# Attention scores over all 128 rows of the array, with high parts of the keys over low parts, and all stages of two tiles

## The chip, the cores and the metric

The kernel runs on one core of one Trainium2 chip. The metric is the device time of one execution in microseconds (us), lower being better. The core's engines, by the short names of the profile, are PE (TensorE; its weight loads are listed apart as PEld), DVE (VectorE), ACT (ScalarE), POOL (GpSimd) and SP (which issues most of the transfers here). A change of about 2% is what a measurement of this kernel can tell from no change.

## The reference

Three layers follow one another on 1536 tokens of width 512 (2 batches of 768 positions, 8 heads of 64).

```python
# 1. attention: local window (n_local = 96) plus the first n_global = 8 keys, with a slope per head
scores = q @ k.T / 8 - slope[h] * dist          # slope[h] = 2 ** -(h + 1); others masked
a = softmax(scores);  attn = a @ v
# 2. gated layer
xn = x / rms(x) * rms_g
x = (silu(xn @ w_gate) * (xn @ w_val)) @ w_out  # float64 weights, 512 x 1536
# 3. one expert of 8 per token
e = argmax(x @ gate);  p = softmax(x @ gate)[e]
out = p * (relu(x @ w1[e]) @ w2[e])             # 512 x 1024, 1024 x 512
```

## The kernel before

**Split numbers.** Products run on PE in a rounded float format. To keep float32 precision an operand is stored as a high part (the rounded value, written by ACT or DVE) and a low part (the value less its high part, written by DVE or POOL). A product is then the sum of three: high by high, high by low, low by high. This holds for the scores (`qt`, `kt`), for the gated layer (`gv`, `ow` are weights, `xn` is the input, `hid` the hidden layer) and for the experts (`ew`, `eh`, `xs`).

**Tiles and stages.** A tile is 128 tokens. `SPLIT` cuts the 12 tiles into stages: three of 2 tiles for the first batch, two of 3 tiles for the second. Attention goes stage by stage, and in a stage by pair of heads (`order`): a group is one stage of one pair, so there are 20 groups. A unit is one tile of a group: 48 units. When the four groups of a stage are done, `tail` normalizes and transposes its tiles (`trx`), and `moe_block(0, ...)` of that stage (its first 3 of 12 slices of the gated layer) may be put between later attention units. After attention the loops `moe_block(1, ...)` (slices 3 to 6) and `moe_block(2, ...)` (slices 7 to 11) run over all stages; the products of a slice (`pg`) take the whole stage as their moving operand, 256 columns wide for 2 tiles and 384 for 3. The last loop ends each stage with `route`, which picks the expert. For the first `NDL` = 4 stages `route` computes its logits on DVE, 16 operations `jk` a tile; for later ones on PE, by transposes `trr` and products `lg`. Then come the experts.

**A group's preparation** (`prep`) is put into the program one group ahead. The natural keys `kn` and queries `qn` lie with the first head of the pair on partitions 0 to 63 and the second on 64 to 127. ACT writes the high keys (line 423), POOL the low keys (line 426; DVE in the first two groups), ACT or DVE the scaled high queries (433 or 429), DVE the low queries (434). POOL then builds with small copies (line 394) the windows with the global keys in front. `kt` and `qt` have two buffers each.

**A unit's scores** (`scores`, line 482) are three products a head, each over the 64 partitions of that head:

```python
seq = list(enumerate(((0, 0), (0, 1), (1, 0))))
r = slice(D * j, D * (j + 1))
lhsT=qt[r, a, t * P:(t + 1) * P], rhs=kt[r, c, ...]
```

DVE adds the distance table to each head's scores and takes the maximum (line 489), ACT takes the exponential (493), PE transposes the result (`pp`, line 504), ACT copies it out of PSUM (512), and PE multiplies it with the values (`xp`, line 533). Meanwhile DVE, ACT and POOL also convert the float64 weights of the gated layer (`cv`, lines 302 to 322).

**Order.** The engines run their queues in program order. A scheduler sets that order when the program is built, from the order of the source and what depends on what; the order below is the built one. `warm` products do no work for the result and are put where PE would idle at the start.

Of the kernel before, what the change touches and what calls it, by code (L numbers as in the profile page):

```python
# [8 lines left out]
F32 = mybir.dt.float32  # L9
F32R = mybir.dt.float32r  # L10
# [3 lines left out]
ACTF = mybir.ActivationFunctionType  # L14
ALU = mybir.AluOpType
# [4 lines left out]
P = 128  # L20
B, H, S, D = 2, 8, 768, 64
NT, DM, DFF = B * S, H * D, 1536
# [23 lines left out]
def kernel(  # L46
# [22 lines left out]
    M0 = [3, 3, 3, 3, 3]  # L69
    M1 = 7  # L70
    PM = [[0, 1, 2], [3, 4, 5, 6], [], [7, 8], [9], [10, 11]]
    NHID = 6
# [59 lines left out]

    gB = const.tile([P, DM], F32, name="gB")
    rg = const.tile([P, KD, NE], F32, name="rg")
    qsc = const.tile([P, NP], F32, name="qsc")
    for hp in range(NP):
        for j in range(2):
            h = 2 * hp + j
            nc.gpsimd.memset(qsc[64 * j:64 * j + 64, hp:hp + 1], 0.125 / slope[h])

    tri_f = const.tile([P, P], F32, name="tri_f")
    nc.gpsimd.memset(tri_f, 1.0)
    nc.gpsimd.affine_select(
# [55 lines left out]
    def load_pair(st, hp, kn, qn, vn):  # L199
        b, t0, nt = STARTS[st] // TB, STARTS[st] % TB, SIZES[st]  # L200
        i0 = 0 if t0 else 1
        nk = nt + 1 - i0
        k0 = (t0 - 1 + i0) * P
        hd = slice(P * hp, P * (hp + 1))
        nc.sync.dma_start(out=kn[:, i0 * P:(nt + 1) * P], in_=kT[b][hd, k0:k0 + nk * P])
        nc.sync.dma_start(out=qn[:, 0:nt * P], in_=qT[b][hd, t0 * P:(t0 + nt) * P])
        nc.sync.dma_start(
            out=rows_of(vn)[:, i0:i0 + nk, 1:P + 1],
            in_=v[b, k0:k0 + nk * P, hd].rearrange("(t p) c -> p t c", p=P),
        )  # L210
        return kn, qn, vn
# [39 lines left out]
    nc.vector.tensor_copy(tab0, tabL[:, P:])  # L251
    nc.vector.tensor_tensor(out=tab0[:, :GW], in0=tab0[:, :GW], in1=gcol, op=ALU.max)
    nc.vector.tensor_tensor(out=tabL[:, :GW], in0=tabL[:, :GW], in1=gcol, op=ALU.max)

    warm(WARM0)
    fast = nc.values_load(flag, min_val=0, max_val=1)

    def body(is_fast):
# [127 lines left out]
        def fast_attention(pool):  # L386
# [9 lines left out]
            def prep(gi):  # L396
                st, hp = order[gi]
                t0, nt = STARTS[st] % TB, SIZES[st]
                i0 = 0 if t0 else 1
                n = nt * P  # L400
                kn, qn, vn = loaded.pop(0)
                vn = rows_of(vn)
                nc.gpsimd.memset(vn[:, i0:nt + 1, 0:VW:VW - 1], 1.0)
                nxt = range(NFP, NFP + 2) if gi == 0 else range(gi + 2, gi + 3) if gi >= NFP else ()
                for gn in nxt:
                    if gn >= len(order):
                        break
                    nat = [
                        pool.tile([P, STAGE if x == "q" else DM if x == "k" else (ST_MAX + 1) * VW], F32, tag=f"{x}n", bufs=2, name=f"{x}n") for x in "kqv"
                    ]  # L410
                    loaded.append(load_pair(*order[gn], *nat))
                qt = pool.tile([P, 2, STAGE], F32R, tag="qt", bufs=2, name="qt")
# [3 lines left out]
                src = kn[:, i0 * P:(nt + 1) * P]  # L416
                khi = kt[:, 0, OW + i0:OW + nt + 1, :].rearrange("p t n -> p (t n)")
                klo = kt[:, 1, OW + i0:OW + nt + 1, :].rearrange("p t n -> p (t n)")
                hi_dve = HI[gi >= HIN]
                if hi_dve[0]:  # L420
                    nc.vector.tensor_copy(khi, src)
                else:
                    nc.scalar.activation(out=khi, in_=src, func=ACTF.Copy)  # L423
# [3 lines left out]
                srq = qn[:, 0:n]  # L427
                if hi_dve[1]:
                    nc.vector.tensor_scalar(
                        out=qt[:, 0, 0:n], in0=srq, scalar1=qsc[:, hp:hp + 1], scalar2=None, op0=ALU.mult  # L430
                    )
                else:
                    nc.scalar.activation(out=qt[:, 0, 0:n], in_=srq, func=ACTF.Copy, scale=qsc[:, hp:hp + 1])
                lo_eng[kq[1]].scalar_tensor_tensor(
                    out=qt[:, 1, 0:n], in0=srq, scalar=qsc[:, hp:hp + 1], in1=qt[:, 0, 0:n].bitcast(F32),
                    op0=ALU.mult, op1=ALU.subtract,
                )
# [12 lines left out]
                mx = pool.tile([P, ST, 2], F32, tag="mx", bufs=3, name="mx")  # L450
                groups.append((st, t0, hp, qt, kt, vn, vx, mx))
# [3 lines left out]
            def scores(g, t):  # L455
                st, t0, hp, qt, kt, vn, vx, mx = groups[g]
                if SB:
                    sb = ps("s", NS, "sp")
                    sp = [sb[:, 0:256], sb[:, 256:512]]
                else:  # L460
                    sp = [ps("s", NS, "sp") for _ in range(2)]
                first = t0 + t == 0
                plain = t0 + t == 1
                n = P if first else 256
                tab = tab0 if first else tabL if plain else tabG
                pr = pool.tile([P, 2, 256], F32, tag="pr", bufs=NPR, name="pr")
                OW = ST_MAX
                seq = list(enumerate(((0, 0), (0, 1), (1, 0))))
                for i, a, c, j in (
                    [(i, a, c, j) for j in range(2) for i, (a, c) in seq] if SB else  # L470
                    [(i, a, c, j) for i, (a, c) in seq for j in range(2)]
                ):
                    r = slice(D * j, D * (j + 1))
                    o = sp[j][:, 0:n]
                    if first:
                        rhs = kt[r, c, OW + 1, :]
                    elif plain:
                        rhs = kt[r, c, OW + t:OW + t + 2, :].rearrange("p t n -> p (t n)")
                    else:
                        rhs = kt[r, c, t:t + OW + 2:OW + 1, :]  # L480
                        o = o.rearrange("p (a n) -> p a n", a=2)
                    mm = nc.tensor.matmul(  # L482
                        out=o, lhsT=qt[r, a, t * P:(t + 1) * P], rhs=rhs, start=(i == 0), stop=(i == 2)
                    )
                un = units.index((g, t))
                if un < WARMU:
                    warm(WARM2[un % len(WARM2)], mm)
                for j in range(2):
                    nc.vector.tensor_tensor_reduce(  # L489
                        out=pr[:, j, 0:n], in0=sp[j][:, 0:n], in1=tab[:, 0:n], scale=-slope[2 * hp + j],  # L490
                        scalar=3.0e38, op0=ALU.add, op1=ALU.min, accum_out=mx[:, t, j:j + 1],
                    )
# [803 lines left out]
```

## Time and profile before

| what | value |
|---|---|
| median of 3 runs | 718.35 us (706.99 to 719.83) |
| the profiled execution | 715.3 us |
| its span, first to last instruction | 713.5 us |
| mean granted clock of TensorE, share of full speed | 0.921 |
| busy: PE, DVE, ACT, POOL | 94%, 63%, 44%, 44% of the span |

The span leaves 1.8 us of the profiled execution outside. A busy share is a mean over stages that differ. A busy PE is not a PE at its peak, since the profile's matmuls overlap and a product waiting inside the array counts as busy.

### The profile page before, as it was taken

The numbers are of one execution on the slowest core, as the hardware profiler recorded it, in microseconds if no ns is written. First come the engines' busy times: TensorE is split into PE (matmuls) and PEld (weight loads), VectorE is DVE, ScalarE is ACT, GpSimd is POOL, SyncE is SP. The second block draws the span as 40 slices with busy tenths as digits, with TensorE's granted clock in tenths as the row PEclk, the third lists the DMA queues.
The fourth block names the chain that finished last, engine by engine and source line by source line (L and its number), as shares of the span: only waits on it lengthen the run. The fifth ranks groups of instructions, "written<-read, shape, count | busy, mean of one in ns | idle before, by whom it ended". The sixth has DMA issues, their size and how long they took to land. (4 is left out here: it accounts for less than half of the span.)

```text
span 713.5 us, 11325 instructions
## 1 busy us (share of the span) xinstructions
PE 669.8 (94%) x4008; PEld 589.9 (83%) x4009; DVE 452.1 (63%) x1249; ACT 312.5 (44%) x594; POOL 310.5 (44%) x343
## 2 busy tenths in 40 slices
PE   7999999999999799999889999988898999999992
PEld 3778988888898698899789999977687888998891
DVE  5667577675479999524447999796546455536410
ACT  2566467675554444222541212131445465555420
POOL 3445444452034555222331323452578586777400
PEclk7555599999999999999999999998999999999997
DMA  6334224140004443200421110233276666676201
GB/s 218 102 109 131 68 72 122 62 145 16 16 8 141 121 145 120 88 0 1 138 99 60 60 60 0 61 87 105 79 262 228 206 221 214 198 230 212 88 12 28
DMA packets 49079, 77.29 MB, mean 108 GB/s; under 512 B 6127, under 2 KB 30703, under 8 KB 49008
## 3 DMA queue, kind: packets, MB, share of 16 engines
q1 hardware_dynamic: 46064, 69.07, 31.1%
q0 software_dynamic: 2944, 7.35, 3.1%
q8 instruction: 35, 0.57, 0.4%
q14 instruction: 36, 0.29, 0.1%
HBM read 70.06 MB, written 7.40 MB: 109 GB/s over the span
## 5 line engine op out<-in xcount | busy, mean ns | idle before, releaser
L701 PE MATMUL pg<-xn,gv 128*128 128x256 f32 (+1 forms) x1440 | 225.1, 311 | 10.2 <-DVE part L747 6.1
L701 PEld LDWEIGHTS pg<-xn,gv 128*128 128x128 f32 x1440 | 213.7, 194 | 15.9 <-DVE part L747 6.7
L738 PE MATMUL po<-ow,hid 128*128 128x512 f32 x432 | 111.2, 406 | 8.1 <-DVE hf L714 3.5
L888 POOL TENSOR_TENSOR ew<-rawe,ew 128x512 fp32r<-128x512 f32 x64 | 99.5, 1568 | 43.0 <-ACT ew L882 42.5
L719 POOL TENSOR_TENSOR hid<-hf,hid 128x256 fp32r<-128x256 f32 (+1 forms) x60 | 57.2, 956 | 122.3 <-ACT hid L718 121.8
L885 DVE TENSOR_TENSOR ew<-rawe,ew 128x512 fp32r<-128x512 f32 x64 | 68.4, 1076 | 65.3 <-ACT ew L882 64.7
L738 PEld LDWEIGHTS po<-ow,hid 128*128 128x128 f32 x432 | 80.9, 193 | 26.2 <-issue 3.8
L942 PE MATMUL py<-ew,eh 128*128 128x512 f32 x384 | 92.7, 399 | 4.1 <-DVE eh L973 3.1
L882 ACT ACTIVATE ew<-rawe 128x1024 fp32r<-128x1024 f32 x64 | 66.7, 1061 | 65.1 <-DMA rawe<-in_moe_w_dram 55.0
L942 PEld LDWEIGHTS py<-ew,eh 128*128 128x128 f32 x384 | 72.4, 191 | 21.3 <-DVE eh L973 3.6
L964 PE MATMUL ph<-xs,ew 128*128 128x256 f32 x672 | 83.3, 282 | 0.8 <-DVE eh L973 0.6
L964 PEld LDWEIGHTS ph<-xs,ew 128*128 128x128 f32 x672 | 81.3, 190 | 1.9 <-DVE eh L973 1.2
L771 DVE CUSTOM_DVE_ANT_0 jk<-part,rgb 128x256 bf16<-128x256 f32 x144 | 71.0, 535 | 0.0
L718 ACT ACTIVATE hid<-hf 128x256 fp32r<-128x256 f32 (+1 forms) x60 | 27.4, 459 | 87.9 <-DVE hf L714 87.8
L493 ACT ACTIVATE pr<-pr,mx 128x256 f32<-128x256 f32 (+1 forms) x96 | 44.7, 484 | 28.5 <-DVE mx L489 26.3
L482 PE MATMUL sp<-kt,qt 64*128 64x256 f32 (+1 forms) x288 | 54.6, 372 | 1.5 <-ACT kt L423 0.8
L322 POOL TENSOR_TENSOR gv<-cv,gv 128x512 fp32r<-128x512 f32 x24 | 31.9, 1335 | 54.6 <-ACT gv L321 54.6
L482 PEld LDWEIGHTS sp<-kt,qt 64*128 64x128 f32 x288 | 38.2, 238 | 17.3 <-DVE mx L489 3.6
L709 ACT ACTIVATE th<-pg 128x256 f32<-128x256 f32 (+1 forms) x60 | 25.1, 420 | 50.7 <-PE pg L701 49.5
L710 DVE SCALAR_TENSOR_TENSOR th<-th,pg 128x256 f32<-128x256 f32 (+1 forms) x60 | 28.0, 468 | 28.4 <-ACT th L709 28.4
L489 DVE CUSTOM_DVE_ANT_0 pr<-sp,tabG 128x256 f32<-128x256 f32 x64 | 26.2, 421 | 27.5 <-PE sp L482 25.6
L504 PE MATMUL pp<-ident,pr 128*128 128x128 f32 x176 | 39.5, 335 | 0.0
(173 smaller groups left out, 867.0 us busy)
## 6 DMA issues: line engine op xcount, KB each, us to landing
rawe<-in_moe_w_dram SPq DMA_DIRECT2D x64, 512.0 KB, 4.0
raw<-in_moe_w_gate_dram SPq DMA_DIRECT2D x12, 512.0 KB, 3.7
raw<-in_moe_w_val_dram SPq DMA_DIRECT2D x12, 512.0 KB, 3.6
raw<-in_moe_w_out_dram SPq DMA_DIRECT2D x12, 512.0 KB, 3.5
x1d<-part SPq DMA_DIRECT2D x12, 256.0 KB, 2.1
kn<-in_k_dram SPq DMA_DIRECT2D x12, 192.0 KB, 2.6
vn<-in_v_dram SPq DMA_DIRECT2D x12, 192.0 KB, 2.6
rawg<-in_moe_w_gate_dram SPq DMA_DIRECT2D x4, 512.0 KB, 4.6
```

What stands on the lines that cost most here:

```text
L482: mm = nc.tensor.matmul(out=o, lhsT=qt[r, a, t * P:(t + 1) * P], rhs=rhs, start=(i == 0), stop=(i == 2))
L493: pin["act"] = nc.scalar.activation(out=pr[:, j, 0:n], in_=pr[:, j, 0:n], func=ACTF.Exp, bias=mx[:, t, j:j + 1], scale=-1.0,)
L504: nc.tensor.transpose(pp[:, (j * nb + a) * P:(j * nb + a + 1) * P], pr[:, j, a * P:(a + 1) * P], ident)
L701: nc.tensor.matmul(out=pg[:, 0:n_], lhsT=gv[:, i, a, kk, :], rhs=x[st][:, kk, :], start=(n == 0), stop=(n == 3 * KD - 1),)
L719: nc.gpsimd.tensor_tensor(out=hh[:, 1], in0=hf, in1=hh[:, 0].bitcast(F32), op=ALU.subtract)
L738: nc.tensor.matmul(out=po, lhsT=hid[mi][:, a, t * P:(t + 1) * P], rhs=ow[:, c, :], start=(mi == 0 and n == 0), stop=(mi == len(ms) - 1 and ...
L771: nc.vector.tensor_tensor_reduce(out=jk, in0=part[i0 + t][:, h * 256:(h + 1) * 256], in1=rgb[h][:, e, :], scale=1.0, scalar=0.0, op0=ALU.m ...
L882: cp = nc.scalar.activation(out=t[:, 0], in_=raw, func=ACTF.Copy)
L885: nc.vector.tensor_tensor(out=t[:, 1, 0:NDV], in0=raw[:, 0:NDV], in1=t[:, 0, 0:NDV].bitcast(F32), op=ALU.subtract)
L888: nc.gpsimd.tensor_tensor(out=t[:, 1, NDV:], in0=raw[:, NDV:], in1=t[:, 0, NDV:].bitcast(F32), op=ALU.subtract)
L942: last_mm["py"] = nc.tensor.matmul(out=py, lhsT=hid(m, a, j), rhs=w2t[m // 2][:, c, (m % 2) * DM:(m % 2 + 1) * DM], start=(n == 0), stop=( ...
L964: nc.tensor.matmul(out=ph[:, 0:CAP], lhsT=w1t[kk][:, a, m * P:(m + 1) * P], rhs=x[:, kk, :], start=(n == 0), stop=(n == 3 * KD - 1),)
```

## The change

The scores of a head use all 128 partitions. Both natural tiles are loaded twice, onto partitions 0 to 63 and again onto 64 to 127, and hold the two heads side by side along the free axis. High keys are written on all 128 partitions, and on the lower 64 of them (64 to 127) the low keys are then written over them. One product of a high query (which stands on both halves) with this column gives high by high plus high by low. The second product is the low query with the same column: it gives low by high, and also low by low, which was left out before. So a head takes two products in place of three, and the pieces are no longer tied to half of the array's rows. Since both heads now share one factor, the queries are scaled by a constant, and a halved copy of each distance table is made for the second head (three ACT operations at the start).

`SPLIT` becomes six stages of 2 tiles, so there are 24 groups and 48 units as before. All `pg` products are 256 wide: 864 of 256 and 576 of 384 columns become 1728 of 256. With `NDL` still 4, `route` works on DVE for 8 tiles (9 before) and on PE for 4 (3 before). Buffers follow: `XT`, `RING` and `FIRST` are rewritten, and the pool `eb` has two buffers in place of three, so that the ring of expert weights keeps twelve.

```diff
-SPLIT = [[2, 2, 2], [3, 3]]
+SPLIT = [[2, 2, 2], [2, 2, 2]]
...
-    XT = "cccss"
-    RING = "ccceewwee"
-    FIRST = [0,1,1,2]
+    XT = "ccccss"
+    RING = "ccceewweec"
+    FIRST = [0, 1, 1, 1, 1]
...
-        nc.sync.dma_start(out=kn[:, i0 * P:(nt + 1) * P], in_=kT[b][hd, k0:k0 + nk * P])
-        nc.sync.dma_start(out=qn[:, 0:nt * P], in_=qT[b][hd, t0 * P:(t0 + nt) * P])
+        for x, src in ((kn[:, 0:2 * nk * P], kT[b][hd, k0:k0 + nk * P]), (qn[:, 0:2 * nt * P], qT[b][hd, t0 * P:(t0 + nt) * P])):
+            for r in range(2):
+                nc.sync.dma_start(
+                    out=x[D * r:D * (r + 1), :].rearrange("d (j s) -> d j s", j=2),
+                    in_=src.rearrange("(j d) s -> d j s", j=2),
+                )
...
+    tabs = []
+    for x in (tab0, tabL, tabG):
+        half = const.tile([P, x.shape[1]], F32, name="half" + str(len(tabs)))
+        nc.scalar.activation(out=half, in_=x, func=ACTF.Copy, scale=0.5)
+        tabs.append((x, half))
...
-                lo_eng[kq[0]].tensor_tensor(out=klo, in0=src, in1=khi.bitcast(F32), op=ALU.subtract)
+                lo_eng[kq[0]].tensor_tensor(out=ks[D:P], in0=src[D:P], in1=ks[D:P].bitcast(F32), op=ALU.subtract)
...
-                seq = list(enumerate(((0, 0), (0, 1), (1, 0))))
-                for i, a, c, j in (
-                    [(i, a, c, j) for j in range(2) for i, (a, c) in seq] if SB else
-                    [(i, a, c, j) for i, (a, c) in seq for j in range(2)]
-                ):
-                    r = slice(D * j, D * (j + 1))
+                for j, a in ((0, 0), (0, 1), (1, 0), (1, 1)):
...
-                        out=o, lhsT=qt[r, a, t * P:(t + 1) * P], rhs=rhs, start=(i == 0), stop=(i == 2)
+                        out=o, lhsT=qt[:, j, a, t * P:(t + 1) * P], rhs=rhs, start=(a == 0), stop=(a == 1)
...
-        ring["pools"] += [(eb, "ew", 3, GV)] * 3
+        ring["pools"] += [(eb, "ew", 2, GV)] * 2
```

The built order shows where the pieces stand. On PE, in the part of attention that has no gated layer beside it yet, the program before has this (`sp` are scores, `pp` transposes):

```order
L504 MATMUL pp<-ident,pr 128x128 x2
L482 MATMUL sp<-kt,qt 128x256 x3
L504 MATMUL pp<-ident,pr 128x128 x4
L482 MATMUL sp<-kt,qt 128x256 x6
L504 MATMUL pp<-ident,pr 128x128 x2
```

And the changed program has this at the corresponding place on PE:

```order
L485 MATMUL sp<-kt,qt 128x256 x2
L507 MATMUL pp<-ident,pr 128x128 x6
L485 MATMUL sp<-kt,qt 128x256 x4
L536 MATMUL xp<-vx,ptS 128x65
L536 MATMUL xp<-vn,ptS 128x65
```

A unit's six score products stood as one piece of six or as two pieces of three (73 pieces for the 48 units); now its four stand as four, or two and two.

On POOL, in the second and third stage, one group's preparation before (the low keys, then windows of keys and values):

```order
L426 TENSOR_TENSOR kt<-kn,kt 128x384
L394 TENSOR_SCALAR kt<-kg 128x2x2x32
L394 TENSOR_SCALAR kt<-kt 128x2x2x96
L403 MEMSET vn 128x3x2
L394 TENSOR_SCALAR vx<-vn 128x260
```

And on POOL in the changed program:

```order
L399 TENSOR_SCALAR kt<-kg 128x2x2x32
L408 MEMSET vn 128x3x2
L399 TENSOR_SCALAR vx<-vn 128x260
L432 TENSOR_TENSOR kt<-kn,kt 64x2x384
L399 TENSOR_SCALAR vx<-vg 32x2x128
L399 TENSOR_SCALAR kt<-kt 128x2x2x96
```

The low keys now are 64 partitions of 768 elements in place of 128 of 384, and stand among the copies of values, with the copy of the windows behind them.

On PE, at the end of the last loop over stages, before: the fourth stage's products and, in the fifth stage's output products `po`, the ranks `rk` of the fourth.

```order
L701 MATMUL pg<-xn_220,gv_3928 128x384 x24
L738 MATMUL po<-ow_3020,hid 128x512 x3
L738 MATMUL po<-ow_3099,hid 128x512 x3
L738 MATMUL po<-ow_3885,hid 128x512 x3
L738 MATMUL po<-ow_3917,hid 128x512
L827 LDWEIGHTS tri
L827 MATMUL rk<-oh,tri 128x16
```

And on PE in the changed program, where the fifth of six stages is routed (`trr`, `lg`) among the sixth one's `pg`:

```order
L831 MATMUL rk<-oh,ones 128x16
L789 MATMUL trr<-ident,part_119 128x128 x4
L704 MATMUL pg<-xn_224,gv_3186 128x256 x12
L789 MATMUL trr<-ident,part_120 128x128 x4
L704 MATMUL pg<-xn_224,gv_4142 128x256 x10
L801 MATMUL lg<-rg,xt 128x8 x4
L704 MATMUL pg<-xn_224,gv_3107 128x256 x12
```

One more stage's logits moved to PE, and `pg` products of the last stage stand between their steps.

## Rows read from the trace of the kernel before

**Rows 1.** Windows: span, busy per engine, granted clock, DMA share, GB/s.

```profile
10.70:89.20 78.50, 77.88 (x336) 61.54 (x335) 51.70 (x169) 44.16 (x97) 33.02 (x56) 0.50 0.41 125
89.20:190.00 100.80, 100.80 (x743) 87.39 (x742) 68.36 (x254) 65.72 (x145) 38.18 (x72) 1.00 0.25 77
190.00:300.00 110.00, 101.44 (x627) 93.77 (x627) 90.67 (x151) 50.15 (x101) 48.12 (x41) 0.97 0.32 101
...
400.00:420.00 20.00, 20.00 (x145) 18.81 (x144) 19.93 (x84) 4.72 (x12) 7.41 (x8) 1.00 0.14 50
```

**Rows 2.** Windows of line 482 alone (scores): span, PE busy, PEld busy, clock, DMA.

```profile
10.70:89.20 78.50, 26.55 (x118) 19.24 (x118) 0.50 0.41 125
89.20:190.00 100.80, 27.72 (x168) 18.79 (x168) 1.00 0.25 77
```

**Rows 3.** Timeline of PE at the half clock: start us, length us, what, count.

```profile
58.44 1.01 PE L482 MATMUL sp<-kt,qt 64*128 64x256 f32 x3
...
62.70 0.63 PE L533 MATMUL xp<-vn,ptS 128*128 128x65 f32 x2
63.13 0.63 PE L504 MATMUL pp<-ident,pr 128*128 128x128 f32 x2
63.69 1.02 PE L482 MATMUL sp<-kt,qt 64*128 64x256 f32 x6
64.64 0.69 PE L504 MATMUL pp<-ident,pr 128*128 128x128 f32 x2
```

**Rows 4.** Timeline of the weight loads there, idle before them in brackets.

```profile
60.42 0.72 PEld L482 LDWEIGHTS sp<-kt,qt 64*128 64x128 f32 x6 [0.33 <-POOL kt L394]
```

**Rows 5.** Timeline of PE at the full clock.

```profile
110.86 0.39 PE L533 MATMUL xp<-vn,ptS 128*128 128x65 f32 x2
111.09 0.61 PE L376 MATMUL trx<-ident,part 128*128 128x128 f32 x4
111.62 0.62 PE L482 MATMUL sp<-kt,qt 64*128 64x256 f32 x6
112.17 0.44 PE L504 MATMUL pp<-ident,pr 128*128 128x128 f32 x2
```

**Rows 6.** Timeline of PE in runs of one kind of product.

```profile
86.54 3.21 PE L701 MATMUL pg<-xn,gv 128*128 128x256 f32 x15
...
302.80 10.39 PE L701 MATMUL pg<-xn,gv 128*128 128x384 f32 x59
...
361.79 10.13 PE L701 MATMUL pg<-xn,gv 128*128 128x256 f32 x84
```

**Rows 7.** Groups by line and form: busy us, mean ns | idle before, releaser.

```profile
L426 POOL TENSOR_TENSOR kt<-kn,kt 128x384 fp32r<-128x384 f32 x12 | 12.9, 1076 | 4.5 <-issue 2.2 <-ACT kt L423 2.0
...
L434 DVE SCALAR_TENSOR_TENSOR qt<-qn,qsc,qt 128x384 fp32r<-128x384 f32 x8 | 6.4, 799 | 0.0
L423 ACT ACTIVATE kt<-kn 128x384 fp32r<-128x384 f32 x12 | 6.3, 522 | 5.6 <-PE sp L482 5.4
...
L426 POOL TENSOR_TENSOR kt<-kn,kt 128x512 fp32r<-128x512 f32 x4 | 5.4, 1362 | 0.7 <-ACT kt L423 0.7
L394 POOL TENSOR_SCALAR kt<-kt 128x384 fp32r<-128x384 f32 x8 | 5.3, 667 | 0.3
L434 DVE SCALAR_TENSOR_TENSOR qt<-qn,qsc,qt 128x256 fp32r<-128x256 f32 x9 | 5.1, 571 | 0.0
...
L433 ACT ACTIVATE qt<-qn,qsc 128x256 fp32r<-128x256 f32 x8 | 3.9, 493 | 0.0
...
L423 ACT ACTIVATE kt<-kn 128x512 fp32r<-128x512 f32 x4 | 2.5, 627 | 1.6 <-PE sp L482 1.6
```

**Rows 8.** Timeline of ACT at the start.

```profile
8.20 1.28 ACT L423 ACT_TABLE_LOAD   x1 [8.06 <-DVE gcol L248]
```

**Rows 9.** The last loop's end: a group (logits on DVE), then the timeline of PE.

```profile
L771 DVE CUSTOM_DVE_ANT_0 jk<-part,rgb 128x256 bf16<-128x256 f32 x144 | 71.0, 535 | 0.0
...
477.46 4.58 PE L738 MATMUL po<-ow,hid 128*128 128x512 f32 x12 [3.54 <-DVE hf L714]
```

More of the change, by code (lines that the diff above doesn't have):

```diff
@@ L65 @@
     NFP, LATE = 3, 8
-    XT = "cccss"
-    RING = "ccceewwee"
-    FIRST = [0,1,1,2]
-    M0 = [3, 3, 3, 3, 3]
+    XT = "ccccss"
+    RING = "ccceewweec"
+    FIRST = [0, 1, 1, 1, 1]
+    M0 = [3] * NSTAGE
     M1 = 7
@@ L134 @@
     rg = const.tile([P, KD, NE], F32, name="rg")
[L135 to L139, printed above, removed]
     tri_f = const.tile([P, P], F32, name="tri_f")
@@ L408, in prep @@
                     nat = [
-                        pool.tile([P, STAGE if x == "q" else DM if x == "k" else (ST_MAX + 1) * VW], F32, tag=f"{x}n", bufs=2, name=f"{x}n") for x in "kqv"
+                        pool.tile([P, 2 * STAGE if x == "q" else 2 * DM if x == "k" else (ST_MAX + 1) * VW], F32, tag=f"{x}n", bufs=2, name=f"{x}n") for x in "kqv"
                     ]
                     loaded.append(load_pair(*order[gn], *nat))
-                qt = pool.tile([P, 2, STAGE], F32R, tag="qt", bufs=2, name="qt")
+                nk = nt + 1 - i0
+                qt = pool.tile([P, 2, 2, STAGE], F32R, tag="qt", bufs=2, name="qt")
                 kt = pool.tile([P, 2, 2 * ST_MAX + 1, P], F32R, tag="kt", bufs=2, name="kt")
@@ L415, in prep @@
                 vx = pool.tile([P, 3, VW], F32, tag="vx", bufs=2, name="vx")
-                src = kn[:, i0 * P:(nt + 1) * P]
-                khi = kt[:, 0, OW + i0:OW + nt + 1, :].rearrange("p t n -> p (t n)")
-                klo = kt[:, 1, OW + i0:OW + nt + 1, :].rearrange("p t n -> p (t n)")
+                src = kn[:, 0:2 * nk * P].rearrange("p (j t n) -> p j t n", j=2, t=nk)
+                ks = kt[:, :, OW + i0:OW + nt + 1, :]
                 hi_dve = HI[gi >= HIN]
                 if hi_dve[0]:
-                    nc.vector.tensor_copy(khi, src)
+                    nc.vector.tensor_copy(ks, src)
                 else:
-                    nc.scalar.activation(out=khi, in_=src, func=ACTF.Copy)
+                    nc.scalar.activation(out=ks, in_=src, func=ACTF.Copy)
                 lo_eng = (nc.vector, nc.gpsimd)
                 kq = KQ0 if gi < KQN else KQ
-                lo_eng[kq[0]].tensor_tensor(out=klo, in0=src, in1=khi.bitcast(F32), op=ALU.subtract)
-                srq = qn[:, 0:n]
+                lo_eng[kq[0]].tensor_tensor(out=ks[D:P], in0=src[D:P], in1=ks[D:P].bitcast(F32), op=ALU.subtract)
+                srq = qn[:, 0:2 * n].rearrange("p (j n) -> p j n", j=2)
+                qhi = qt[:, :, 0, 0:n]
                 if hi_dve[1]:
                     nc.vector.tensor_scalar(
-                        out=qt[:, 0, 0:n], in0=srq, scalar1=qsc[:, hp:hp + 1], scalar2=None, op0=ALU.mult
+                        out=qhi, in0=srq, scalar1=0.125 / slope[2 * hp], scalar2=None, op0=ALU.mult
                     )
                 else:
-                    nc.scalar.activation(out=qt[:, 0, 0:n], in_=srq, func=ACTF.Copy, scale=qsc[:, hp:hp + 1])
+                    nc.scalar.activation(out=qhi, in_=srq, func=ACTF.Copy, scale=0.125 / slope[2 * hp])
                 lo_eng[kq[1]].scalar_tensor_tensor(
-                    out=qt[:, 1, 0:n], in0=srq, scalar=qsc[:, hp:hp + 1], in1=qt[:, 0, 0:n].bitcast(F32),
+                    out=qt[:, :, 1, 0:n], in0=srq, scalar=0.125 / slope[2 * hp], in1=qhi.bitcast(F32),
                     op0=ALU.mult, op1=ALU.subtract,
@@ L489, in scores @@
                     nc.vector.tensor_tensor_reduce(
-                        out=pr[:, j, 0:n], in0=sp[j][:, 0:n], in1=tab[:, 0:n], scale=-slope[2 * hp + j],
+                        out=pr[:, j, 0:n], in0=sp[j][:, 0:n], in1=tab[j][:, 0:n], scale=-slope[2 * hp],
                         scalar=3.0e38, op0=ALU.add, op1=ALU.min, accum_out=mx[:, t, j:j + 1],
```

8 lines of the change are left out of this document (4 added, 4 removed).

## The prediction

> **What bounds the kernel now.** I read the windows by stage first, then the time under the score line alone, then PE's timeline around single pieces of scores, and last the groups of the operations that the change makes longer.
>
> The windows say PE everywhere up to 190 us. From 10.7 to 89.2 it is busy 77.88 of 78.5 us at a granted clock of 0.50, which is the 1.2 GHz level, and from 89.2 to 190 it is busy throughout at 1.00, the 2.4 GHz level [rows 1]. The reader should see beside it that DVE and ACT have room there: DVE 51.70 and ACT 44.16 us of the first stretch (66% and 56%), 68.36 and 65.72 us of the second (68% and 65%). So in both a microsecond less on PE can become a microsecond less of time, until DVE or ACT take over.
>
> The scores hold PE for 26.55 us of the first stretch and 27.72 us of the second [rows 2]. 120 products, 20 units, run in the first (two of them just before its window); the second has all 168 of the other 28 units. The time busy is not all that a piece costs, so I take single pieces. At the half clock a pair of transposes ends at 63.13 + 0.63 = 63.76, then come six score products, and the next pair of transposes ends at 64.64 + 0.69 = 65.33 [rows 3]. Transposes and value products follow each other at 0.215 us there (two from 62.70 to 63.13), so the six cost 1.57 - 0.43 = 1.14 us. At the full clock four transposes end at 111.70 and the pair behind the scores at 112.61; with a pitch of 0.115 us (two from 110.86 to 111.09) the six cost 0.91 - 0.23 = 0.68 us, say 0.69 [rows 5]. The piece of three at 58.44 has the length of the piece of six, 1.01 and 1.02 us [rows 3]. This is the main point: a unit that the built order splits into two pieces of three pays twice. The two heads' products of a six overlap in the two halves of the array; the three of one head have no partner.
>
> **Scores, the term that carries the forecast.** The built order before has 73 pieces. The 20 units at the half clock make 27 of them, one being twelve long and counted as two; less two for the first short ones, which stand among idle products, that is 26 x 1.14 = 30 us. The other 46 make 46 x 0.69 = 32 us. After, a unit is four products over all rows. Such products of 256 columns take 3.13 / 15 = 0.21 us at the half clock (86.54 to 89.67, its length less the overlap of the last) and 10.13 / 84 = 0.12 us at the full one [rows 6]. No row shows what splits cost these; they have the shape of their neighbours, whose pieces follow without a gap, so I take nothing. 20 x 4 x 0.21 = 17 us and 28 x 4 x 0.12 = 13 us. PE is relieved of 13 + 19 = 32 us, if clocks stay as they were.
>
> The idle 0.33 us of the weight loader ahead of the piece at 60.42 [rows 4] is part of that cost, beside a wait on POOL that the row names. The Trainium skill (TensorEngine Tiling (Array Packing), Key Properties) says that changing the tiling mode drains the engine, which would be such a gap at every piece.
> **What is lost of it to the other engines.** Each group's conversion of keys and queries now has twice the elements per partition. ACT's high keys go from 0.522 (384 elements) to 768, by the step of 0.105 from 384 to 512 an estimate of 0.84 us; its high queries from 0.493 to about 0.70; DVE's low queries from 0.571 (256) by the step of 0.228 to about 1.03 [rows 7]. In the first stretch, 10 groups, that is 10 x 0.46 = 4.6 us more on DVE and about 10 x 0.53 = 5.3 us on ACT. In the second, 2 groups of two tiles and 8 of three become 14 of two: low queries from 2 x 0.57 + 8 x 0.80 = 7.5 to 14.4 us, and on ACT the high parts from about 11 to 21 us (the first groups of a batch 0.63 in place of 0.52). DVE then has 56.3 us in 78.5 - 13 = 65.5, 86%, and in the second stretch 75.3 in 100.8 - 19 = 81.8, 92%, with ACT near it. How full DVE can be before PE waits has two bounds in the rows. From 400 to 420 us DVE is busy 19.93 of 20 while PE never stops: all 32 us are kept. From 190 to 300 DVE is at 82% and PE at 101.44 of 110 [rows 1]: at 82% the stretches would last 69 and 92 us and the gain is 10 + 9 = 19. Attention alternates between PE, DVE and ACT in every unit, as the conversions and hidden layers of 190 to 300 do, so I am nearer to the second: **23 us**.
>
> **POOL and the loads.** The low keys cost 1.076 us for 128 partitions of 384 elements and 1.362 for 512 [rows 7]. For 64 of 768 no row exists: with the number of elements it stays 1.08, with the length of a partition it becomes 1.93. I take 1.93. POOL is busy 33.02 of 78.5 us and 38.18 of 100.8 [rows 1], so 0.86 x 24 us is covered in sum; what is behind it in a group, the copy of the windows, is the rival of the chain. Two loads more a group, and twice the bytes of q and k, stand against a DMA share of 0.41 and 0.25 there: nothing, unless a group's tiles come late; the bound on the other side is inside the same rival.
>
> **The smaller terms.** Stages: 576 products of 384 columns at 10.39 / 59 = 0.176 us become 864 at 0.12 [rows 6], 101 to 103 us: +2. The twelfth tile routed on PE adds 4 transposes and 8 small products at the pitch of 0.115: +1.4. The start: three halved tables, about 0.4 us each by ACT's 0.4 to 0.5 for 256 columns, stand before the first key conversion, but the table load of 1.28 us at 8.20 [rows 8] can then run earlier, while ACT waits for the tables; the first pair's loads issue two later. From -0.5 to +2, I take +1. The last loop: PE waits 3.54 us at 477.46 for a hidden layer that DVE had queued behind the fourth stage's logits [rows 9]. There are 16 of these operations fewer, 16 x 0.49 = 8 us, and `pg` of a sixth stage lies between. I take -3 from a range of -4 to +4, because PE now also waits for the fifth stage's `route` in its own queue.
>
> **The sum.** 715.3 - 23 + 2 + 1.4 + 1 - 3 = **694 us**. The profiled execution lies 3 us below the median of the three runs and 8 above the fastest, within the 2% that a measurement of this kernel tells from no change (704 us and above is not told apart from the median).
>
> **Rivals.** *All of it arrives*: DVE and ACT fill up as from 400 to 420 us, 715.3 - 32 + 1.4 = 685 us. If the clock also rises earlier than at 89.2, the first stretch is bound by DVE's 56.3 us instead and ends some 6 us sooner still: 679. [...]
>
> *The other engines take over sooner*: with them no fuller than 75%, the stretches last 75 and 100 us, the gain is 4 and the time 713; midway to the forecast 707. The same would come from conversions that run slower beside a longer POOL operation.
>
> *The chain of preparation, the other side*: with two buffers, a group's keys can only be written when the scores of the group before the last are done. Then follow high keys 0.84, low keys 1.93, the windows 0.67 [rows 7] and a copy or two in front of each, some 5 to 6 us in all. Cover is PE's work on the group between: two units of 4 x 0.21 + 8 x 0.215 = 2.56 us each, 5.1 us at the half clock, and at the full clock half of that and what stands between of the gated layer, on average 81.8 / 14 = 5.8. If 24 groups wait 1.3 us each, the 32 us are gone; at 2 us each the time is 715.3 - 31 + 48 = 732. Before, a group of three tiles had longer cover and 1.2 us less chain.
>
> *Three passes were fewer than four*: where the two heads' products overlap, a unit needs three passes of the array before and four now. If all pieces did so at no other cost, the scores would take 20 x 0.21 + 28 x 0.12 = 8 us more, and the time would be 715.3 + 8 + 1 = 724. The pieces of six do overlap, 1.02 us for six against 1.01 for three [rows 3]; but with the pieces of three the 48 units made 73 pieces, and either piece costs more than four passes, 1.14 against 0.84 and 0.69 against 0.48 us. That is why I give it little. The Trainium skill (TensorEngine Tiling (Array Packing), Theoretical Speedup) gives up to twice the rate to a contraction of 64 rows or less; by that rule the change loses, and the trace bears it out in the pieces of six alone.
>
> **Chances.** Forecast, 688 to 702 us: 0.48. All of it: 0.25. Sooner full: 0.17. The chain: 0.08. Three passes: 0.02. Leaving out a tenth at either end gives 677 to 714. Faster by over 2%: the first two but for a little, 0.71. Within 2%: 0.20. Slower: 0.09.
>
> **What would show it.** Scores as pieces of four with a pitch of 0.21 and 0.12 us, no idle weight loader ahead of them, and some 40 us busy under their line in place of 54 (30 of pitches, and 0.2 for the overlap at the end of each of some 60 pieces). Attention's end, now 190 us, near 168. DVE and ACT above 80% busy up to there. 256-wide `pg` at 0.12 us throughout. The forecast is wrong if the high keys of a group are followed by waits of PE for the windows (the chain), if the clock is full from early on, or if PE's gaps between 190 and 300 us grow by what was won before.

## The result, and the profile after

| | before | after | ratio, 95% interval |
|---|---|---|---|
| first comparison | 714.8 us (706.99 to 719.83, 4 executions) | 690.8 us (690.1 to 691.12, 4) | 0.9754 [0.9712, 0.9795] |
| again, beside the experiments | 706.9 us (698.97 to 719.66, 13) | 691.8 us (689.26 to 692.66, 4) | 0.9825 [0.9764, 0.9885] |

Medians are over all executions; the ratios here and below leave out executions more than 1.5% above the fastest of their kernel, which cuts the long ones of the kernel before and, below, of runs 1, 3 and 6. The changed kernel is faster by 2.5% in the first comparison, near the forecast of 694 us. In the second it is faster by 1.8% (1.2 to 2.4), which does not clear the 2% that a measurement of this kernel can tell. The kernel before is less steady: its 62 later executions, on four chips, took 697.8 to 723.4 us, with medians of 705.8 to 707.4.

The profiled execution after took 690.83 us (span 689.1, mean granted clock 0.953). Windows by stage, in the columns of [rows 1]:

```profile
10.70:89.20 78.50, 67.26 (x379) 59.52 (x380) 64.45 (x200) 53.38 (x113) 49.88 (x67) 0.72 0.72 186
89.20:190.00 100.80, 95.08 (x736) 89.80 (x735) 82.92 (x280) 73.12 (x160) 52.40 (x79) 0.98 0.40 106
190.00:300.00 110.00, 105.24 (x705) 95.18 (x705) 84.53 (x138) 43.51 (x92) 48.56 (x43) 0.98 0.33 101
```

Three things differ from [rows 1]. PE is no longer full up to 190 us: it idles 11 us of the first stretch and 6 of the second. DVE has risen to 82% in both, ACT to 68% and 73% (the prediction had it near DVE in the second), and the DMA share of the first from 0.41 to 0.72. And the granted clock of the first stretch is 0.72 where it was 0.50: in parts of it PE ran at 2.4 GHz. Line 485 alone (the scores; same columns as [rows 2]):

```profile
10.70:89.20 78.50, 26.75 (x94) 19.44 (x94) 0.72 0.72 186
89.20:190.00 100.80, 20.47 (x98) 14.75 (x98) 0.98 0.40 106
```

In sum that is 47 us, where the prediction expects some 40 in place of 54; a busy time includes products that wait inside PE. The timeline of PE shows a piece by itself, at the full clock, between products of the gated layer:

```profile
82.41 0.36 PE L704 MATMUL pg<-xn,gv 128*128 128x256 f32 x1
82.61 0.40 PE L485 MATMUL sp<-kt,qt 128*128 128x256 f32 x2
82.84 0.88 PE L704 MATMUL pg<-xn,gv 128*128 128x256 f32 x6
```

From the end of the first row (82.77) to that of the last (83.72) are 0.95 us, and the six `pg` take 6 x 0.119 = 0.71 of them: two scores cost 0.24 us, two passes and nothing else. A piece of six cost 0.68 before, and one of three took as long [rows 3, 5].

What PE waits for in attention, the five largest (12 to 180 us; us in total, times, longest):

```profile
PE sp L485 <- DVE mx L492: 5.6, 11, 1.7
PE sp L485 <- POOL kt L399: 4.0, 3, 1.5
PE sp L485 <- DVE kt L432: 2.1, 1, 2.1
PE xp L536 <- DVE part L546: 1.8, 2, 1.0
PE trx L381 <- DVE part L374: 1.5, 1, 1.5
```

The waits are for the maxima of the unit before, for the windows that POOL builds last in a group, and once, at 12.0 us, for the first low keys. The groups that answer to [rows 7]:

```profile
L432 POOL TENSOR_TENSOR kt<-kn,kt 64x768 fp32r<-64x768 f32 x16 | 31.4, 1964 | 5.8 <-POOL kt L399 3.2 <-issue 1.7
L442 DVE SCALAR_TENSOR_TENSOR qt<-qn,qt 128x512 fp32r<-128x512 f32 x21 | 24.6, 1172 | 2.3 <-ACT qt L441 2.2
L429 ACT ACTIVATE kt<-kn 128x768 fp32r<-128x768 f32 x16 | 13.5, 842 | 6.1 <-PE sp L485 5.3 <-PE pg L704 0.4 <-issue 0.3
L441 ACT ACTIVATE qt<-qn 128x512 fp32r<-128x512 f32 x20 | 12.4, 621 | 1.7 <-DMA qn<-in_q_dram 1.6
```

The last loop's end, on PE, where [rows 9] showed a wait of 3.54 us for DVE:

```profile
446.48 0.18 PE L830 MATMUL rk<-oh,tri 128*128 128x16 bf16 x1 [1.95 <-DVE oh L823]
...
463.77 1.22 PE L704 MATMUL pg<-xn,gv 128*128 128x256 f32 x9
464.83 7.30 PE L741 MATMUL po<-ow,hid 128*128 128x512 f32 x30
```

The last `po` now run without a wait; there is a wait of 1.95 us for the fourth stage's choice of experts.

### The profile page after: what moved, and what is told of

Its sections match the earlier page's. It is cut to its first block, busy times and chain, and to the rows that moved or that the text cites. A ratio compares the mean times of both kernels' runs of the same rounds, so it can differ in the third digit from the quotient of the medians.

```text
span 689.1 us, 11953 instructions
## 1 busy us (share of the span) xinstructions
PE 637.0 (92%) x4214; PEld 574.1 (83%) x4215; DVE 456.8 (66%) x1276; ACT 324.6 (47%) x631; POOL 338.6 (49%) x355
## 5 line engine op out<-in xcount | busy, mean ns | idle before, releaser
L704 PE MATMUL pg<-xn,gv 128*128 128x256 f32 x1728 | 229.0, 286 | 7.0 <-DVE hf L717 3.6
L722 POOL TENSOR_TENSOR hid<-hf,hid 128x256 fp32r<-128x256 f32 x72 | 59.0, 824 | 119.9 <-ACT hid L721 119.6
L721 ACT ACTIVATE hid<-hf 128x256 fp32r<-128x256 f32 x72 | 29.8, 415 | 82.3 <-DVE hf L717 82.2
L774 DVE CUSTOM_DVE_ANT_0 jk<-part,rgb 128x256 bf16<-128x256 f32 x128 | 59.4, 507 | 0.0
L485 PE MATMUL sp<-kt,qt 128*128 128x256 f32 (+1 forms) x192 | 47.2, 351 | 12.0 <-DVE mx L492 5.6
L485 PEld LDWEIGHTS sp<-kt,qt 128*128 128x128 f32 x192 | 34.2, 227 | 18.0 <-DVE mx L492 5.8
L712 ACT ACTIVATE th<-pg 128x256 f32<-128x256 f32 x72 | 26.8, 376 | 44.1 <-PE pg L704 42.7
L713 DVE SCALAR_TENSOR_TENSOR th<-th,pg 128x256 f32<-128x256 f32 x72 | 29.6, 414 | 26.8 <-ACT th L712 26.8
L432 POOL TENSOR_TENSOR kt<-kn,kt 64x768 fp32r<-64x768 f32 (+1 forms) x21 | 38.0, 1811 | 8.8 <-issue 4.0
L316 DVE SCALAR_TENSOR_TENSOR cv<-raw,cv 128x512 uint32<-128x512 uint32 x36 | 35.8, 997 | 0.5
```

What stands on the lines that cost most here:

```text
L432: lo_eng[kq[0]].tensor_tensor(out=ks[D:P], in0=src[D:P], in1=ks[D:P].bitcast(F32), op=ALU.subtract)
L485: mm = nc.tensor.matmul(out=o, lhsT=qt[:, j, a, t * P:(t + 1) * P], rhs=rhs, start=(a == 0), stop=(a == 1))
L704: nc.tensor.matmul(out=pg[:, 0:n_], lhsT=gv[:, i, a, kk, :], rhs=x[st][:, kk, :], start=(n == 0), stop=(n == 3 * KD - 1),)
L722: nc.gpsimd.tensor_tensor(out=hh[:, 1], in0=hf, in1=hh[:, 0].bitcast(F32), op=ALU.subtract)
L774: nc.vector.tensor_tensor_reduce(out=jk, in0=part[i0 + t][:, h * 256:(h + 1) * 256], in1=rgb[h][:, e, :], scale=1.0, scalar=0.0, op0=ALU.m ...
```

## The experiments

Twelve kernels ran, each beside the kernel before (medians 707.4, 706.9, 706.6 and 705.8 us in the four batches: runs 1 to 4, 5 to 8, 9 to 11, 12). "After" below is the 691.8 us of run 5.

**1. The stages alone** (`XT`, `RING`, `FIRST`, `M0` and `eb` as changed too; scores as before).

```diff
-SPLIT = [[2, 2, 2], [3, 3]]
+SPLIT = [[2, 2, 2], [2, 2, 2]]
```

> The kernel before with the six stages of two tiles alone (SPLIT, XT, RING, FIRST, M0 and the two buffers of eb as changed); scores still three products a head over 64 rows. My theory, that the 9 us won behind the last loop and the 4 us lost in the loops belong to the stages, and the 19 us of attention to the scores: 710 us, ratio to the kernel before 0.990 to 0.997, attention ends near 196 us as before, the last loop's end comes some 9 us less behind the last pg than before. Rival, that the scores brought the end's gain too (engines less full when the loop begins): 716 to 720 us, ratio 1.002 or more.

Measured: 709.3 us (699.52 to 717.19), ratio 0.9989 [0.9923, 1.0055]. No difference; my expectation of -5 us falls. The end of the last loop is the new one, in this kernel's timeline too:

```profile
477.82 1.98 PE L701 MATMUL pg<-xn,gv 128*128 128x256 f32 x16
479.64 7.35 PE L738 MATMUL po<-ow,hid 128*128 128x512 f32 x30
```

From the last `pg` to the last `po` are 7.2 us, against 19.9 in the trace of before and 7.1 after. So the short end does belong to the stages, but the loops ahead of it are 11 us longer (from the last value product of attention to the last `pg` 289.6 us, before 278.3): what was won at the end was spent on the way. So the gain is the scores', 17.5 us by the medians (709.3 to 691.8). Run 1's executions spread widely; by the ratios, 0.9989 against 0.9825, it is some 12 us.

The last value product of attention, in the traces of the kernel before, of this one and of the changed one, and the first stretch of this one:

```profile
195.20 0.39 PE L533 MATMUL xp<-vn,ptS 128*128 128x65 f32 x2
...
189.80 0.39 PE L533 MATMUL xp<-vn,ptS 128*128 128x65 f32 x2
...
178.39 0.39 PE L536 MATMUL xp<-vn,ptS 128*128 128x65 f32 x2
...
10.70:89.20 78.50, 75.64 (x400) 60.83 (x398) 57.92 (x195) 49.68 (x111) 37.03 (x60) 0.69 0.42 129
```

Attention ends at 195.6, 190.2 and 178.8 us. The first two have the same scores, but in the first stretch the granted clock was 0.50 [rows 1] in the one and 0.69 in the other.

**2. A third product a head in the changed kernel.**

```diff
-for j, a in ((0, 0), (0, 1), (1, 0), (1, 1)):
+for j, a, i in ((0, 0, 0), (0, 1, 1), (0, 1, 2), (1, 0, 0), (1, 1, 1), (1, 1, 2)):
```

> The changed kernel with a third product a head: the low query's product stands twice, so the scores have a small error. PE gets 96 more passes of 256 columns, 40 x 0.215 + 56 x 0.119 = 15 us; nothing changes for the other engines. If PE still sets attention's pace (my theory: most of what PE saves arrives), the time rises by 10 to 15 us, to 701 to 706, attention ends 189 to 194 us. If DVE, ACT or the preparation on POOL set it now, PE has room for them and the time rises by at most 5 us, to 696 or less.

Measured: 702.0 us (697.4 to 705.83), ratio 0.9997 [0.9951, 1.0043]: 10 us above after (12 by the ratios). PE still sets much of the pace: some two thirds of the 15 us arrive, or more.

**3. The products over 64 rows again.**

```diff
-for j, a in ((0, 0), (0, 1), (1, 0), (1, 1)):
+for j, a in ((0, 0), (1, 0), (0, 1), (1, 1)):
+    r = slice(D * j, D * (j + 1))
-    rhs = kt[:, j, ...];  lhsT=qt[:, j, a, ...]
+    rhs = kt[r, j, ...];  lhsT=qt[r, j, a, ...]
...
-lo_eng[kq[0]].tensor_tensor(out=ks[D:P], in0=src[D:P], in1=ks[D:P].bitcast(F32), op=ALU.subtract)
+lo_eng[kq[0]].tensor_tensor(out=ks[D:P], in0=src[D:P], in1=one[D:P] ..., op=ALU.mult)
```

> The changed kernel with its two products a head taken over 64 rows again (head 0 on rows 0 to 63, head 1 on 64 to 127), and the operation of the low keys writes the value times one, which is the high key once more, at the same size; the product with the low keys is left out. Passes fall from four a unit to two where the heads overlap; the other engines do the same work. Theory, that each piece of half-height products between full-height ones costs about 0.5 us at the half and 0.33 at the full clock beyond its passes: pieces of two or four cost 0.93 and 0.57 us in place of 0.43 and 0.24 a product pair, PE gets some 15 us more, the time is 698 to 706. Rival, that only passes count: PE gets some 6 us less, the time is 684 to 691, and pieces take 0.43 and 0.24 us.

Measured: 711.5 us (700.76 to 714.99), ratio 1.0015 [0.9925, 1.0105]. The height of the products gives the whole gain back: by the ratios it is 13 us slower than after, inside my range; by the median it is 20 us slower and above the range. Not all else stayed the same: POOL's operation with a constant as its second input got shorter (1.96 us after), and the first score starts at 10.1 us in place of 12.0. Both can only have helped the time.

```profile
L434 POOL TENSOR_TENSOR kt<-kn,one 64x768 fp32r<-64x768 f32 x16 | 23.9, 1491 | 4.6 <-POOL kt L401 2.5 <-issue 1.1 <-ACT kt L431 0.2
```

PE's timeline, first at the half, then at the full clock:

```profile
64.15 0.63 PE L513 MATMUL pp<-ident,pr 128*128 128x128 f32 x2
64.72 0.80 PE L491 MATMUL sp<-kt,qt 64*128 64x256 f32 x4
65.44 0.69 PE L513 MATMUL pp<-ident,pr 128*128 128x128 f32 x2
...
139.82 0.40 PE L710 MATMUL pg<-xn,gv 128*128 128x256 f32 x2
140.15 0.51 PE L491 MATMUL sp<-kt,qt 64*128 64x256 f32 x4
140.59 0.44 PE L513 MATMUL pp<-ident,pr 128*128 128x128 f32 x2
...
147.52 0.38 PE L710 MATMUL pg<-xn,gv 128*128 128x256 f32 x1
147.83 0.50 PE L491 MATMUL sp<-kt,qt 64*128 64x256 f32 x2
148.26 0.74 PE L710 MATMUL pg<-xn,gv 128*128 128x256 f32 x4
```

Worked out as above, at the full clock the piece of four (two heads, overlapped) costs 0.81 - 0.23 = 0.58 us and the piece of two (one head) 1.10 - 0.48 = 0.62: both are two passes (0.24) and some 0.35 us more. At the half clock the piece of four costs 1.35 - 0.43 = 0.92, two passes (0.43) and 0.49 more. So a piece of half height among others has a price of its own beside its passes, the same for two products and for four; for the six of before, three passes where the heads overlap, it is 0.68 - 0.36 = 0.32 at the full clock.

**4. Without the low keys on POOL.**

```diff
-lo_eng[kq[0]].tensor_tensor(out=ks[D:P], in0=src[D:P], in1=ks[D:P].bitcast(F32), op=ALU.subtract)
-scale=0.125 / slope[2 * hp]
+scale=0.0625 / slope[2 * hp]
```

> The changed kernel without the operation of the low keys on POOL (1.96 us a group, 22 groups, and two on DVE); the high keys stand on both halves, and the queries are scaled by half of the constant, so the product with the low keys is left out. If the chain of preparation (high keys, low keys, windows) or POOL beside DVE holds the scores back, the part of PE's 32 us that did not arrive in attention (13 us) comes back in good part: 677 to 684 us, waits of PE for POOL's windows gone, DVE's low queries near 0.7 us in place of 1.17. If other things hold them back (DVE and ACT full, the loads): 688 to 692 us.

Measured: 680.5 us (677.75 to 683.05), ratio 0.9623 [0.9528, 0.9719], 11 us below after. Its window from 75 to 176 us, and DVE's low queries up to 190 us:

```profile
75.00:176.00 101.00, 99.45 (x803) 95.47 (x803) 81.52 (x313) 79.29 (x178) 34.19 (x75) 1.00 0.45 122
```
```profile
L442 DVE SCALAR_TENSOR_TENSOR qt<-qn,qt 128x512 fp32r<-128x512 f32 x21 | 14.7, 699 | 2.8 <-ACT qt L441 2.8
```

From 75 us on PE is nearly full again (in run 5 it is busy 94.92 us of that window), and the low queries fall from 1172 ns to 699 with no change of their own. Of the 11 us, 1.9 come at the start, where the low keys on DVE are left out too: the first score starts at 10.2 us, after at 12.0. Up to 75 us PE still idles, and one wait of 3.1 us for POOL's windows stays, which I had expected to go. Some 9 us of what had not arrived of PE's saving hang on POOL's operation; by its place in the chain, by its slowing DVE, or by both.

**5. The changed kernel again.**

> The changed kernel itself once more, beside the kernel before on the same chip as the experiments, so that each experiment has a time of the changed kernel next to it. Expected: 688 to 692 us as in the first result; the kernel before took 707 us here in the median of the first batch, so a ratio of 0.975 to 0.98. A ratio nearer to 1 than 0.985 would mean that part of the first difference came from single executions of the kernel before with a long half clock.

691.8 us as told above: the smaller gain is the kernel before taking 707 us here. The ratio of 0.9825 lies a little above the range I expected.

**6. Low keys half on DVE, half on POOL** (one operation a head).

```diff
-lo_eng[kq[0]].tensor_tensor(out=ks[D:P], in0=src[D:P], ...)
+for j in range(2):
+    (nc.vector, nc.vector if gi < KQN else nc.gpsimd)[j].tensor_tensor(out=ks[D:P, j], in0=src[D:P, j], ...)
```

> The changed kernel with the low keys of the pair's first head on DVE and those of the second on POOL, side by side (in the first two groups both on DVE, as it is). POOL's operation falls from 1.96 to about 1.0 us, DVE gets 22 x 0.5 = 11 us more, and its low queries stand beside POOL's operation for half the time. Theory, that the chain of preparation and the slower DVE beside POOL's operation hold back what is missing: 683 to 688 us. Rival, that DVE is full: 691 to 697 us.

Measured: 702.0 us (695.47 to 707.7), ratio 0.9941 [0.9888, 0.9995]: worse than either expectation. PE waited 11.3 us for the maxima in attention, and the mean clock of the ten executions was 0.943. Why sharing is worse than either engine alone is open.

**7. All low keys on DVE.**

```diff
-KQ = (1, 0)
+KQ = (0, 0)
```

> The changed kernel with all low keys on DVE. 64 partitions of 512 took 0.69 us there, so 768 take about 1.0: 22 us more on DVE, less the 10 us by which its low queries are longer beside POOL's operation; POOL loses 42 us, and the chain of a group is 1 us shorter. Theory of the chain and of POOL's operation beside DVE: 683 to 689 us, low queries near 0.70 us. Rival, that DVE's sum sets the pace of attention: 693 to 700 us.

Measured: 692.4 us (687.62 to 695.89), ratio 0.9862 [0.9799, 0.9924]; as after. PE's waits from 12 to 180 us for POOL's windows fall to 0.7 us, and the largest is

```profile
PE sp L485 <- DVE mx L492: 7.5, 11, 1.5
```

It was 5.6 us in the trace after.

**8. Three buffers for the natural tiles** (and smaller tiles, so that they fit).

```diff
-pool.tile([P, ... 2 * DM if x == "k" ...], tag=f"{x}n", bufs=2)
+pool.tile([P, ... 2 * (ST_MAX + 1) * P if x == "k" ...], tag=f"{x}n", bufs=3)
-vx = pool.tile([P, 3, VW], ...)
+vx = pool.tile([P, ST_MAX, VW], ...)
```

> The changed kernel with three buffers in place of two for the natural keys, queries and values (the key tile cut to the 768 elements that it needs, the window tile of the values to two windows, so that they fit). The loads of a group then need not wait until an earlier group's low keys are written. POOL stands 20 us before values that have not landed, up to 190 us, with the low keys behind it in its queue. If these waits are part of the chain: 684 to 688 us, and POOL's waits for the values nearly gone. If they only fill time that POOL has: 689 to 692 us.

Measured: 691.0 us (689.97 to 694.43), ratio 0.9831 [0.9766, 0.9897]. POOL's waits for values fell by a third (10.1 + 11.0 us up to 190 us, 20.5 + 10.9 in run 5), and the time did not move. But POOL now waited 15.0 us for PE's value products before it could write the windows of the values, so its queue gained little: earlier loads alone bring nothing, and what they would bring with more window tiles was not tried.

**9. POOL's operation kept, its result to a tile that nothing reads.**

```diff
-vx = pool.tile([P, 3, VW], ...)
+vx = pool.tile([P, ST_MAX, VW], ...)
+side = pool.tile([P, 2, ST_MAX + 1, P], ..., bufs=1)
...
-lo_eng[kq[0]].tensor_tensor(out=ks[D:P], ...)
+lo_eng[kq[0]].tensor_tensor(out=side[D:P, :, 0:nk], ...)
-scale=0.125 / slope[2 * hp]
+scale=0.0625 / slope[2 * hp]
```

> The changed kernel with POOL's operation of the low keys kept at its size, but written to a tile that nothing reads; the high keys stand on both halves and the queries are scaled by half of the constant, so the product with the low keys is left out. The chain of a group (high keys, windows) no longer contains the 1.96 us, while POOL is as busy and runs the same kind of operation beside DVE. If the chain held back the 10 us that came when the operation was left out: 679 to 685 us, DVE's low queries still near 1.1 us. If it was DVE being slower beside POOL's operation, or POOL's own time: 687 to 693 us.

Measured: 701.3 us (697.02 to 703.78), ratio 0.9951 [0.9915, 0.9986]. The experiment doesn't part what it was to part: POOL's timeline shows that the windows still stand behind the operation in its queue.

```profile
137.13 2.22 POOL L433 TENSOR_TENSOR side<-kn,kt 64x768 fp32r<-64x768 f32 x1
139.44 0.83 POOL L399 TENSOR_SCALAR kt<-kt 128x384 fp32r<-128x384 f32 x1
```

That it is slower than after goes in part with the clock. PE's timeline and the window behind it:

```profile
92.26 0.44 PE L486 MATMUL sp<-kt,qt 128*128 128x128 f32 x2
95.21 0.79 PE L486 MATMUL sp<-kt,qt 128*128 128x256 f32 x2 [2.52 <-DVE mx L493]
```
```profile
94.80:115.30 20.50, 20.09 (x96) 20.09 (x96) 12.95 (x53) 12.83 (x30) 7.48 (x14) 0.50 0.44 112
```

PE waited 2.52 us, and for the next 20.5 us the granted clock was 1.2 GHz with PE full: at most 10 us lost there. Why it stayed low that long here and not after other waits is open. Nor is the clock all of it: executions of this kernel with a mean clock of 0.947 and 0.954 took 699.6 to 700.7 us, those of run 5 at 0.946 to 0.951 took 689.3 to 692.7.

**10. Without DVE's low queries** (`scale` halved as in run 9).

```diff
-lo_eng[kq[1]].scalar_tensor_tensor(out=qt[:, :, 1, 0:n], ...)
-lhsT=qt[:, j, a, ...]
+lhsT=qt[:, j, 0, ...]
```

> The changed kernel without DVE's low queries (24.6 us of DVE in attention); the second product takes the high query again, both at half of the constant, so the products with the low queries are left out. PE's and POOL's work and the chain of the keys stay. If DVE's sum sets the pace of attention: 676 to 683 us, with PE's waits for the maxima (5 us) nearly gone. If the chain of the keys on POOL does: 687 to 692 us.

Measured: 687.3 us (684.81 to 691.31), ratio 0.9791 [0.9723, 0.9858]. 24.6 us less on DVE bring 4.5 us in the median, and the interval overlaps that of after. So DVE's sum sets the pace in small part at most. With the low queries gone POOL's operation can't hold them up either, so that delay, too, costs no more than these 4.5 us. PE's waits for POOL's windows and low keys stay (3.8 and 1.4 us).

**11. More warm products.**

```diff
-WARM2, WARMU = (1, 0), 12
+WARM2, WARMU = (1, 1), 24
```

> The changed kernel with a warm product (128 rows, 512 columns, no use for the result) behind the scores of each of the first 24 units, in place of every other one of the first 12: 18 more, 0.43 us each at the half and 0.21 at the full clock, 4 to 8 us of PE, part of it in time in which PE waits. If the clock falls in attention because PE waits there, it stays at the full level for longer between 12 and 75 us, and the time is 684 to 690 us. If the half clock there has nothing to do with it: 692 to 698 us.

Measured: 692.3 us (689.61 to 695.02), ratio 0.983 [0.9768, 0.9892]. No difference in time; the mean clock was 0.953 to 0.963 (the eight executions of after: 0.946 to 0.959), so useless products behind the scores raised it little, if at all.

**12. Queries before keys.**

```diff
+nc.scalar.activation(out=qhi, in_=srq, ...);  lo_eng[kq[1]].scalar_tensor_tensor(out=qt[:, :, 1, 0:n], ...)
 nc.scalar.activation(out=ks, in_=src, ...);  lo_eng[kq[0]].tensor_tensor(out=ks[D:P], ...)
-nc.scalar.activation(out=qhi, in_=srq, ...);  lo_eng[kq[1]].scalar_tensor_tensor(out=qt[:, :, 1, 0:n], ...)
```

> The changed kernel, complete, with a group's queries converted ahead of its keys (ACT: high queries, then high keys). DVE's low queries (0.69 us alone, 1.17 in the mean beside POOL's low keys) can then run before POOL's operation starts; the chain of the keys gets 0.62 us longer. If DVE being slower beside POOL's operation is a good part of what was lost: low queries near 0.75 us, DVE 9 us less in attention, 684 to 688 us. If the chain of the keys counts more: 693 to 697 us. If neither sets the pace: 689 to 692 us.

Measured: 692.7 us (689.37 to 696.44), ratio 0.9813 [0.9768, 0.9858]. The low queries fell to 905 ns, 19.0 us in sum for 24.6, and the time stayed. No complete kernel of these beats the changed one.

## Why the prediction was right, and where not

- **The scores, the main term.** The mechanism is shown by run 3: a piece of half height costs its passes and some 0.5 us at the half, 0.35 at the full clock, so pieces of three (1.14 and 0.69 us) cost more than four full passes, and the pieces after cost 0.24 us for two. That the heads' products overlap, and that this does not pay for it, are both in its rows. The rule of the Trainium skill (TensorEngine Tiling (Array Packing), Key Properties) that a change of mode drains the engine agrees with these rows; its "Up to 2×" for 64 rows (Theoretical Speedup) is reached within a piece only, and run 3, which has no more passes than after, and half of them where a piece holds both heads, is 20 us slower by the medians and 13 by the ratios.
- **What of it arrives: 23 forecast.** Run 1 to run 5 is 17.5 us by the medians and 12 by the ratios, each with 2 us of later start in it, so 14 to 20 arrive: at or below the lower bound of 19, not the 23 chosen. In the traces attention's end moves by 16.8 us from before to after, but 5.4 of them are there in run 1 already, whose scores are the old ones and whose clock was higher; from run 1 to after it moves by 11.4, 13.4 with the later start. The forecast end "near 168" took the last score, 186.9 before and 169.1 after, for the end.
- **The reason for the loss was half wrong.** I priced it by how full DVE is. DVE did reach 82%, the bound that gives 19. But 24.6 us less on DVE brought 4.5 us in the median, inside the intervals (run 10), while POOL's 1.96 us operation, left out, brought 11, 1.9 of them at the start (run 4). Moving that work to DVE (7), loading earlier (8) or starting DVE earlier (12) brought nothing, and sharing it (6) cost 10. So the group's preparation on POOL, the mechanism of my rival "the chain", is in it, at a smaller size: 6 us of PE's waits in attention name the low keys or POOL's windows, 2.1 of them at the start. That it holds up DVE's low queries accounts for some 4.5 us at most (run 10), and shorter low queries brought nothing (run 12). Whether the rest is the chain, POOL's queue or other DVE operations that it holds up is not settled, since run 9 did not part them.
- **Durations.** Low keys 1.96 us (1.93 estimated by the length of a partition), high keys 0.84 (0.84), high queries 0.62 (0.70). Low queries: 1.03 estimated, 0.69 alone and 1.17 in the mean. I had no term for an operation that is slower beside another engine's, only a clause in a rival.
- **The clock.** I held the clock fixed, and put its earlier rise into a rival at 679 us. It did rise within the first stretch (0.72 for 0.50), and the time was still 691, because PE then waits for the others. And the base was an execution with a long half clock: 715.3 us, where the median of 62 others is near 707. The forecast gain of 21 us was nearer to the first pair's 24 than to the 15 of the second. That 694 came so near is therefore partly luck: the scores brought less than the 23 us forecast, and the long half clock of the base made up for it. From 707 us the same terms would have given 686.
- **Smaller terms.** Stages, routing and last loop, +2 + 1.4 - 3 = +0.4 in sum: run 1 shows no difference, but of larger parts, 9 us won at the end (12.7 less 15 `po` of the third tile at 7.30 / 30 = 0.243 us) and, in run 1, nearly 8 lost in the loops (11.3 less the same 15 `po`). Start, +1: it was +2, and not by the halved tables, which end before ACT's first key conversion at 9.4 us as before; the first score waits for low keys on DVE, which stand behind low queries there.
- **Rivals.** "Three passes were fewer than four" is excluded by run 3. "All of it arrives" and "sooner full" would have been 685 and 707 to 713.

## What to carry to other kernels

Price a matmul over part of the rows by what it costs between its neighbours, from end to end in the timeline, not by its passes: here two products of half height cost as much as five of full height at the full clock. When an engine that is full is relieved, look for the next one in the chain of each group, and test it by leaving an operation out before moving it: moving the low keys to DVE changed nothing here and sharing them cost 10 us, while leaving them out gained 11. And where executions of a kernel differ by 3%, take several before choosing the base of a forecast.

## What the runs showed of the hardware that was not expected

**A DVE operation waits for POOL's.** In the trace after, the same operation takes 0.68 us without POOL's low keys beside it and 2.23 with them:

```profile
117.35 0.68 DVE L442 SCALAR_TENSOR_TENSOR qt<-qn,qt 128x512 fp32r<-128x512 f32 x1
...
134.72 2.23 DVE L442 SCALAR_TENSOR_TENSOR qt<-qn,qt 128x512 fp32r<-128x512 f32 x1
```
```profile
134.30 2.10 POOL L432 TENSOR_TENSOR kt<-kn,kt 64x768 fp32r<-64x768 f32 x1 [1.71 <-issue]
```

POOL ends at 136.40, DVE at 136.95, 0.55 us later and so nearly its own 0.68 us. The Trainium skill (SBUF — State Buffer, SBUF: two separate sides) says that a DVE operation with two inputs in SBUF and a GpSimd operation that reads SBUF exclude each other for a whole instruction; by that rule, DVE would end at 136.40 + 0.68 = 137.08, and the trace agrees to 0.13 us.

**The granted clock goes with the spread.** In the 13 executions beside run 5, the kernel before takes 699.0 us at a mean clock of 0.950 and 719.7 at 0.916; the changed one stays at 0.946 to 0.951 there and within 3.4 us. Kernels with scores of half height spread widely (run 1: 699.5 to 717.2, run 3: 700.8 to 715.0), the changed kernel hardly. Full height alone does not keep an execution steady, though: runs 6 and 9 took 695.5 to 707.7 and 697.0 to 703.8. Run 2, with 96 more full-height products than after, has mean clocks of 0.951 to 0.969, although it is 10 us longer. At a mean clock of 0.95 the two kernels differ by about 10 us, 699 to 702 against 689 to 692: by this estimate some 5 of the 15 us between the medians come with the clock.
